# Another order of five engines' work in a kernel of gated linear attention and a feed-forward layer

## The chip, the cores and the metric

The kernel runs on one core of one Trainium2 chip. A core has five engines, each with its own instruction queue that runs in order: TensorE (PE, matmuls into PSUM), VectorE (DVE), ScalarE (ACT, activations by table), GpSimd (POOL) and SyncE (SP, which here only issues transfers). ACT can issue transfers too. The engines wait for one another through semaphores. The metric is the device time of one execution in microseconds.

## The reference

A linear attention with a complex decay, over 4 batches, 8 heads, 768 steps and heads of 48, and then a feed-forward layer over 3072 tokens of 384 with a hidden width of 2048:

```python
scale = np.minimum(mag, 0.999) / (mag + 1e-06)       # mag = |a|
for t in range(S):
    S_re, S_im = ar*S_re - ai*S_im + k[t] v[t]^T, ar*S_im + ai*S_re
    y[:, :, t] = np.einsum('bhd,bhde->bhe', q[:, :, t], S_re)
h = x @ w_in                                          # x: y with the heads side by side
g = h * np.tanh(softplus(h))
return g @ w_out
```

## The kernel before

The work is cut into 12 units of 256 tokens (three to a batch), each unit into two chunks "a" and "b" of 128. A unit goes through three stages.

*Elementwise* (`elementwise`, from line 330 on): loads R and I (the parts of a), Q, K and V. It takes size, logarithm and angle of a, sums them along time (by matmuls with a triangular matrix in units 0 and 1, "mag sum" and "phase sum", lines 404 to 414; by scans on DVE in later units), and forms exp, sine and cosine. "size" (L465) adds two squares, "slope" is L466, "turns" rounds the phase. "grow" multiplies q and k by the magnitudes, "turn sin" and "turn cos" (L545) by sine and cosine. Then twelve relays (L552, six a chunk: sin0 to sin2 and cos0 to cos2) move X and QK through DMAs into T, where heads lie as the matmuls want them.

*Attention* (`attention`): per chunk "kn" (transposes, L608) with "kn out" (L613), "am" (q times k, L620) with "am out" (the mask, L627, DVE only), "y" (L638) with "y out" (L643), "hold" (L668) and "pd" (L651) with "S add" for the state. Then "x move" (L701) brings y by DMA to x, and from unit 1 on "xH" (L712) and "xL" (L717) split it into two parts.

*Feed-forward* (`moe`): eight pairs of 256 hidden columns a unit. For a pair, "mm1" (L746) makes ph, then exp, cap (L815), square, ln, inv on ACT and DVE, "gate" (L759), "gh" (L765) and "gl" (L771) on ACT and DVE, and "mm2" (L783) adds to po. "o" (L794 on ACT, L796 on DVE) scales the result, and "store" writes it. Unit 0 has plain float32 products in four groups of two pairs, q0 to q3, for each chunk; later units use three products of split operands. PSUM banks are few: three for ph, two for pa (am, kn, pd and the sums share them), two for po.

*Weights*: w0 to w15 come in packed words of 768 KB each (w_in even, w_out odd), three buffers at a time, so the load of w3 waits until w0 is unpacked, and so on. "low", "shift" (L283), "join" (L287) and "carry" (L291) unpack one on ACT and DVE; "high" (L309) and "rest" (L314) split it for unit 1 on.

*Fillers*: 40 operations "spin" (numbers 72 to 111) of two matmuls each (L844) that work on the mask alone and whose result nobody reads.

All of this is first listed as 2434 numbered operations, each with the engines that may run it (`op("AV", name, f)`: the first letter is the default). Then `issue` runs through the list `ORDER`, which gives the sequence of all operations; a letter behind a number (V, A, G, T, S for DVE, ACT, POOL, PE, SP) chooses another engine than the default. Each engine gets its operations in this sequence, and the semaphores follow from the data. So `ORDER` alone sets what stands behind what in every queue: also behind which wait a DMA issue stands on SP. The core of it:

```python
for i, other in order:
    engines, name, f = self.ops[i]
    e = other or engines[0]
    assert e in engines
```

Numbers that come up below: 7, 10, 11 and 12 are unit 0a's two squares, size and slope, 24 to 29 those of 0b; 49 and 53 "u0a turn sin" and "turn cos", 50 to 52 and 54 to 56 its relays; 65 to 67 and 69 to 71 those of 0b; 116 and 118 "u0a am0" and "am1"; 154 and 156 "u0b am out0" and "am out1"; 157 and 158 "u0b y0" and "y1"; 192 + 5i is the load of w of index i, and the next four are its low, shift, join and carry, so that 217 to 221 are those of w5; 566 is the load of V2, 597 to 609 are unit 2's relays.

Of the kernel before, what the change touches and what calls it, by code (L numbers as in the profile page):

```python
# [59 lines left out]
361A 152V 175 160 156 157 176 219 150 569 158 214 356 573 163 161 220 164 172 162 272 213V 360A 357 215 159 358 190  # L60
273 221V 189 216V 191 177 274 165 188 359 575 227 178 275 576 363 276 224 223 366 578 283 277 367 180 362 225 369A 370
282 278 364 226V 232 292 284 365 181 279 179 368 228 572 293 237 375A 182 285 303 371 229 183 230 286 280 376A 372 374
574 234 281 373 231V 287 235 386 242 388 131 302 233V 387 236V 288 389 390 289 446 247 378 392 444 239 290 294 381 391
304 379 295 380A 393 312 238 240 296 291 244 297 305 241V 298 394 430 382 395 442 377 245 385 243 397 383 249 400 248
401 384 299 577 398 246V 252 744 448 300 402 399 306 250 307 313 579 438 251V 308 322 396 580 262 452 565 403 405 314
257 323 404 254 564 253 583 255 406 407 582 315 256 309 409 581 408 436 301 410 594A 316 584 411 317 264 318 412 585
265 263 414 413 586 417 324 418 319 434 415 325 587A 266V 310 420 432 259 423 588 593A 326 333 422 751 431 267 258 421
332 260 743 590 566 424V 342 433 428 327 429 334 592 343 328 589 320 335 425 329 426 311 435 591 427 336 321 596 337
462 269 597 603 463 338 602 344 600 748 330 339 607 268 345 604 331 261V 346 599 749 419 606 270 474 347 605 416 440
340 271V 598 464 601 752 348 475 456 437 458 341 465 349 466 439 756 610 612 350 613 441 476 352 443 486 611 353 467  # L70
609 754 351 750 445 468 753G 757 614 354V 469 454 355 616 932 615 470A 933 498 477 758 608 447 478 487 471 479 595 449
499 480 488 617 621 450 481 619 746 937 759 622 745 618 489 760 490 623 491 761 626 620 500 472 492 482 762 501 511
459 755 483 473 624 493 510 763 451 484 494 453 522 502 764 940 628 625 512 460V 503 523 765 627 504 513 630 629 514
505 515 631 495 524 766 485 632 455 636 767A 496 747 516 525 635 768 526 535 936 527 517 633 497 771 773 634 774A 775A
528 534 506 518A 547 507 536 529 770 546 530 641V 519 508 639V 637 537 772 777 509 538 520 539 531 779 521 640 778 638
642 780 938 532 784 548 643 540 549 785 541 533 550 781 542 551 461 783 644 552 787 457 939 655 786 645 769 543 788
656 942 790 789 553 544 944 1123 776 554 657 953 545 646 555 941 791 793 647 556 943 648 557 792V 794 945 658 954 795
558 649 560V 559 797 946 955 1124 796 782 650 668 659 935 947 948 667 956 561 660 934 949 957A 680 661 651 798 679 669
1128V 1131 802 662 1129 652 804 681 670 799 803 671 805 800 682 806 950 683 808 807 692 684 672 809V 653 958 673 952
810 674 951 1132 812 965A 811 1130 654 961V 685 959 1134 691 801 813 703 693 686 663A 675 815 960 964 1133 814 664 963  # L80
817 962 819 1135 694 716 818 816 967 695 825 704 696 824 715 676 969 974 970 665 697 1136 666 820 975 705 698 687A 822
677 706 717 966 1144 688 823 707 678 1145 977 830 708 976 728 699A 968 709 727 979 1137 710 972 718 689 978 821 719
700 1138 971 690 828V 973 711 729 1139 826 981 1305 831 720 983 980 827 701 829 721 1304 730 1140 731 702 1146 722 832
712 723A 1125 1141 833 1126 844 724 1143 1147 713 834 732 1148 714 984 982V 733 1149 725 1142 835 734 985 1155 1151V
735A 987 986 1152 736 857 1153 845 1150 726 988 836 1312 1309V 737 1154A 846 1157 738 992 739 741V 837 994 740 993
1160 847 838 856 995 1158 848 1156 996 1310 839 1494 997 990 998V 858 840A 859 989 1164 849 999 860 1001 1311 1168 850
868 1314G 861 1169 851 869 1159 1000V 841 1165 881 870 1167 1002 991 742 880 1316 1163 1161 1003 1170 1008 862 1166
1004 1005 1493 1009 871 1313 1006 872 863 1010 873 852 1317 1315 892 874 1011 1171 882 1012G 875 1173 1318 893 1007V
1320 1014 904 883 894 1162 853 1319 905 1013 884 1321 1016 885 842 1306 895 864A 1322 1015 843 1498 1307 886 854 1127
1325 876A 1021 855 865 1499 887 1017 866 1019 888 896 877 906 867 1022 897 1018 1326 1020 917 907 1327 908 878 909  # L90
1172 916 898 1328A 899 879 1174 889 1323 1175 910 1177 918 1176 1501 919 1023 1178 900A 1502G 920 1024 1500 921 1179
1503 1506 1180 1504 1324 1182 1329 1507 1184 911 1332 890 901 922 912 1025 1334 891 1335A 1333 902 1185 1330 1026 903
923 1336A 1331 913 1035 924A 1685 1183 1338 1027 1048 1505 914 925 1514 1345 1036 915 1037 1509 1684 1508 1038 1339
926 1186 1039 1515 1350 1028 927 1340 1510 1029 1351 1047 928 1348 930 1030 1040 1187 1516 929 1517 1049 931 1189 1342
1041 1031 1518A 1347 1032 1059 1181V 1349 1519 1343 1060 1341 1188 1033 1344 1050 1042 1051 1346 1034 1511 1061 1043A
1072 1062 1512 1071 1190 1052 1689V 1191 1044 1063 1053 1192 1064 1054 1352 1520 1055 1193 1692V 1354 1690 1045 1196
1197 1065 1693 1083 1513 1195 1066 1194 1073 1084 1074 1067 1075 1046 1085 1086 1096 1056 1087 1202V 1076 1095 1200V
1198V 1337 1068 1077 1495 1057 1088 1201 1496 1203 1526A 1089 1078 1308 1058 1525A 1199 1097 1353V 1107 1098 1090 1099
1069 1695 1355 1100 1079 1697 1108 1080 1101 1356 1109 1698 1358 1357 1691 1522V 1204 1110 1091A 1524 1523 1205 1070
1359 1694 1111 1081 1521 1102 1361 1699 1360 1363 1365 1364 1206 1082 1112 1366 1092 1103A 1207 1216 1113 1528 1208  # L100
1367 1696 1369 1093 1114 1529 1527 1535 1217 1115A 1362 1094 1368 1104 1537 1209 1229 1370V 1865 1534 1105 1540 1218
1539 1106 1219 1116 1220 1705 1210 1228 1117 1118 1371 1119 1121V 1211 1120 1373 1122 1372 1230 1538 1241 1231 1866
# [968 lines left out]
```

## Time and profile before

| | us |
|---|---|
| median of 3 timed runs (592.98 to 595.51) | 594.56 |
| the profiled execution | 597.63 |
| its span, first to last instruction | 595.9 |
| busy in it: PE | 582.5 |
| ACT | 476.2 |
| DVE | 464.2 |
| POOL | 20.9 |
| share of the 16 DMA engines, main queue | 36.8% |

The span is that of one execution under the profiler. "Busy" is the union of an engine's instructions. An instruction's time is from its start to its end, and neighbours overlap: nine matmuls of mm1 listed at some 281 ns each go by in 1.06 us. "Idle before, releaser" tells how long the engine had stood still ahead of an instruction, and whose semaphore ended that. "Granted clock" is the share of its full clock that PE was given in a stretch. The transfers of one queue are issued in order, about 0.6 us apart on SP, and run side by side once issued.

### The profile page before, as it was taken

To read this page: it belongs to the slowest core of one execution; us is meant where nothing else is said; L and a number is where in the kernel's file an instruction comes from. 1 tells how busy PE (TensorE), PEld (TensorE's weight loads), DVE (VectorE), ACT (ScalarE), POOL (GpSimd) and SP (SyncE) were. 2 spreads that over 40 slices of the span, in tenths; PEclk is the share of its full clock that TensorE was granted. 3 is DMA by queue.
4 is the path that set the end of the run, shared out by engine and by line. 5 is a ranking of instruction groups with operands and counts; after the bars stand their busy time and mean duration, and the time that the engine had idled before them with its cause. 6 is when DMAs were issued, how large, how long until landed. Compare 5 with 4: busy or idle time off the path is not lost.

```text
span 595.9 us, 11915 instructions
## 1 busy us (share of the span) xinstructions
PE 582.5 (98%) x4654; PEld 551.1 (92%) x4654; DVE 464.2 (78%) x823; ACT 476.2 (80%) x766; POOL 20.9 (4%) x37
## 2 busy tenths in 40 slices
PE   8979999999999999999999999999999999999995
PEld 4669788799999999999999999999999999999995
DVE  5888999999999977998578889966887646356351
ACT  8877999999998998978868768968977666565572
POOL 4010010100000010000000000001000000000000
PEclk9999999999999999999999999999999999999998
DMA  8595875414606353153270072072053160001000
GB/s 298 185 286 156 252 258 168 152 55 122 181 25 180 94 144 110 49 156 91 72 221 2 15 204 76 14 202 80 28 170 99 36 190 16 28 2 28 28 0 33
DMA packets 57248, 67.07 MB, mean 113 GB/s; under 512 B 4832, under 2 KB 50272, under 8 KB 57184
## 3 DMA queue, kind: packets, MB, share of 16 engines
q1 hardware_dynamic: 55664, 65.01, 36.8%
q10 hardware_dynamic: 1520, 1.22, 0.8%
q8 instruction: 39, 0.64, 0.4%
q14 instruction: 25, 0.20, 0.1%
HBM read 37.75 MB, written 4.72 MB: 71 GB/s over the span
## 4 chain that ended last, share of the span: by engine, by line
PE 58%; DVE 16%; ACT 12%; DMA 6%; issue 4%; SPq 3%; POOL 0%; DVEq 0%; ACTq 0%; POOLq 0%
PE po L783 22%; PE ph L746 21%; ACT e L172 5%; PE ypsum L638 4%; PE pa L620 4%; PE pd L651 3%; ACT X L172 3%; DMA words<-w_out 3%; DVE g L759 2%; SPq L552 2%; DMA T<-X 2%; PE pkn L608 1%; DVE QK L545 1%; DVE X L545 1%; PE junk L844 1%
## 5 line engine op out<-in xcount | busy, mean ns | idle before, releaser
L172 ACT ACTIVATE e<-e 128x512 f32<-128x512 f32 x192 | 118.2, 627 | 26.4 <-DVE e L815 24.6
L746 PE MATMUL ph<-xH,wh 128*128 128x256 f32 x462 | 132.6, 287 | 0.0
L746 PE MATMUL ph<-xL,wh 128*128 128x256 f32 x462 | 129.7, 281 | 0.0
L746 PE MATMUL ph<-xH,wl 128*128 128x256 f32 x462 | 129.7, 281 | 0.0
L783 PE MATMUL po<-wh,gh 128*128 128x384 f32 x308 | 106.4, 345 | 0.0
L783 PE MATMUL po<-wh,gl 128*128 128x384 f32 x308 | 104.4, 339 | 0.0
L783 PE MATMUL po<-wl,gh 128*128 128x384 f32 x308 | 104.1, 338 | 0.0
L759 DVE SCALAR_TENSOR_TENSOR g<-e,ph 128x512 f32<-128x512 f32 x96 | 65.2, 681 | 40.5 <-ACT e L172 40.0
L746 PEld LDWEIGHTS ph<-xH,wh 128*128 128x128 f32 x462 | 87.1, 189 | 0.6
L746 PEld LDWEIGHTS ph<-xL,wh 128*128 128x128 f32 x462 | 87.0, 188 | 0.5
L746 PEld LDWEIGHTS ph<-xH,wl 128*128 128x128 f32 x462 | 87.0, 188 | 0.0
L172 ACT ACTIVATE e<-ph 128x512 f32<-128x512 f32 x96 | 56.4, 590 | 35.9 <-PE ph L746 29.7
L771 DVE TENSOR_TENSOR gl<-g,gh 128x512 fp32r<-128x512 f32 x88 | 60.2, 686 | 14.4 <-PE po L783 9.5
L172 ACT ACTIVATE e<-e,fifth 128x512 f32<-128x512 f32 x96 | 68.9, 720 | 1.2
L815 DVE TENSOR_SCALAR e<-e 128x512 f32<-128x512 f32 x96 | 40.0, 419 | 25.6 <-ACT e L172 25.4
L783 PEld LDWEIGHTS po<-wh,gh 128*128 128x128 f32 x308 | 57.9, 188 | 0.4 <-issue 0.4
L783 PEld LDWEIGHTS po<-wh,gl 128*128 128x128 f32 x308 | 57.9, 188 | 0.3 <-DVE gl L771 0.2
L783 PEld LDWEIGHTS po<-wl,gh 128*128 128x128 f32 x308 | 57.9, 188 | 0.0
L170 ACT ACT_TABLE_LOAD x42 | 53.9, 1283 | 0.7
L620 PE MATMUL pa<-T 96*128 96x128 f32 x384 | 48.7, 276 | 0.4 <-DMA T<-X 0.4
L620 PEld LDWEIGHTS pa<-T 96*128 96x128 f32 x384 | 46.2, 191 | 1.3 <-issue 0.8
L627 DVE TENSOR_TENSOR am<-pa,cmask 128x512 f32<-128x512 f32 x48 | 32.7, 685 | 10.3 <-PE pa L620 10.1
(138 smaller groups left out, 1053.1 us busy)
## 6 DMA issues: line engine op xcount, KB each, us to landing
T<-X SPq DMA_DIRECT2D x68, 129.0 KB, 2.7
T<-QK SPq DMA_DIRECT2D x68, 129.0 KB, 2.5
words<-w_in SPq DMA_DIRECT2D x8, 768.0 KB, 6.5
words<-w_out SPq DMA_DIRECT2D x8, 768.0 KB, 7.1
QK<-k SPq DMA_DIRECT2D x12, 384.0 KB, 5.2
QK<-q SPq DMA_DIRECT2D x12, 384.0 KB, 4.4
V<-v SPq DMA_DIRECT2D x12, 384.0 KB, 4.8
R<-a_re SPq DMA_DIRECT2D x12, 384.0 KB, 3.9
```

The lines of the kernel that those rows point to most:

```text
L170: self.nc.scalar.preload_act_table_set(need)
L172: return self.nc.scalar.activation(out, in_, func, **kw)
L545: e.tensor_tensor(both(st[dst], g)[..., :C], both(st["QK"], g)[..., :C], t.unsqueeze(2).broadcast_to([P, t.shape[1], 2, C]), ALU.mult)
L620: e.matmul(d["pa", g][:, i, :], T()[:, 4 * g + i, 1, :C], T()[:, 4 * g + i, 0, :C], start=True, stop=True)
L627: e.tensor_tensor(d["am", g], d["pa", g], cmask.unsqueeze(1).broadcast_to([P, 4, C]), ALU.mult)
L638: e.matmul(ypsum[64 * par:64 * par + D, i, :], lhs, rhs, start=m == 0, stop=first or m == 1)
L651: e.matmul(d["pd", g][:, i, :], d["kn"][:, h, :], st["V"][:, c, h * D:(h + 1) * D], start=not held, stop=not held or i == 3)
L746: e.matmul(ph[k][:, slot(k, j, a), :], win(x, j, kt, a), st[y][:, kt, cols(k)], start=n == 0, stop=n + 1 == len(todo))
L759: e.scalar_tensor_tensor(g_[k], e_[k], 2.5, ph[k], ALU.subtract, ALU.mult)
L771: e.tensor_tensor(gs[k][1], g_[k], gs[k][0].bitcast(F32), ALU.subtract)
L783: e.matmul(po[t], x[:, slot(k, j, a), 0 if halved else t * P:C if halved else (t + 1) * P], wout(y, j, a), start=j == 0 and a == 0 and n == 0,
L815: op("V", f"{n} cap", lambda e, k=k: e.tensor_scalar_min(e_[k], e_[k], math.exp(20.0)))
```

## The change

The list `ORDER` is another permutation of the same 2434 operations. Nothing else differs. The new list comes from a search that took the service time of every transfer as 1.3 times what a trace had shown. 170 of the operations are given to another engine than before (75 from ACT to DVE, 63 from DVE to ACT, 14 from POOL to DVE, 7 from DVE to POOL, 5 from ACT to POOL, and three DMA issues each way between SP and ACT). The diff replaces the whole list; its beginning, which holds the start of unit 0, and its end:

```diff
 ORDER = [(int(x.rstrip("VAGTS")), x.lstrip("0123456789")) for x in """
-72 0 1 73 2 127 74 3 75 128 7V 5 8 76 4 9 10 77 192 12 11G 197 78 24V 202 13 79 80 132V 25 81 166V 82 27V 19 14 28G 83
-22 15 84 167 85 133 86 169V 16 17 87 170G 135V 26 18 31 32 29G 134 23 88 21 89 20 90 46A 91 33 136 92 42 137 93 94 34
-45 35 30 43V 193 194 95 47A 195 44 96 37 97 49 98 99 196V 50 100 168 36 51 53 139 38 199 55A 56 101 62 60 102 140 54
-103 61A 52 39 104 40 105 6 48 204 57 106 207 41 107 200 138 562 108 58 64 116 59 141 203V 112 114 205 118 117 67A 109
-63 68 110 66A 120 65A 119 69 71A 113V 121 563 206V 115 123 70A 198V 125 217 122 209 111 142 124 210 185A 143 208 126
-201V 187A 144 171 184A 212 567V 129 146 149 211V 145 186 147A 153 570V 130 568 148 151 222 218V 173 155 571G 154 174
...
-2404 2416 2405A 2422 2394 2384 2423 2424 2395 2406 2425 2426 2396 2417A 2427 2407 2418 2428 2408 2429A 2419 2430 2336
-2420 2431 2432 2433A
+72 0 1 73 127 4 74 128 75 2 7 3 76 8 10V 5 11 77 192 14 197 78 9 202 15 12 79 16 132V 80 17 133 81 13 82 83 18 24V
+166V 25 135V 84 19 20 85 22 134 86 27V 21 28 87 88 46 23 31 89 136 32 90 45 167 91 26 92 33 93 29 42 137 34 47A 30 43V
+49 44 36 139 194 53 94 35 39 56 48 140 40 168 54 169V 193V 95 38 51 96 199 142 97 50 41 200 37 98 57 52 99 62 195 100
+55 101 6 60 102 203 562 103 171 104 58 196V 105 61A 138 106 172 64 207 116 59 204 67A 112 68 114 66A 118 117 70A 69
+107 205 71A 563 120 113 119 65A 123 206V 198 108 115V 217 141 170 125 567V 121 124 201V 109 173 143 122 126 212 209
+185A 208V 144 186A 210 146 211V 145 149 184A 153 147 570 148 110 150V 174 155 63 154 187A 129 360G 219 151 176 130 157
+361 156 568 220 158 152 569 571 160 159 111 218V 575 163 190 573 164 222 175 161 213V 188 576 214 273 189 356 165 215
...
+2421 2415 2405A 2384 2423 2424 2395 2406 2425 2416 2396 2417A 2426 2407 2418 2427 2408 2428 2429 2419 2430 2336 2420
+2431 2432 2433A
 """.split()]
```

Per engine, read off the two lists: on PE 148 of the 615 places hold the same operation, and no operation of unit 0 or 1 stands more than nine places from where it was among PE's first 120. SP's queue around unit 2's relays was 597, 602, 600, 607, 604, 599, 606, 605, 598, 601 and is 598, 597, 605, 606, 599, 604, 608, 609, 932, 566, 600, 602, 607, 353, 601.

More of the change, by code (lines that the diff above doesn't have):

```diff
@@ L63 @@
[L63 to L102, printed above, removed]
@@ new lines @@
+891 1178 901 1500 1035 1026 1334 1182 1027 1179 1503G 1336A 1183 1332 1180 920 1335A 1028 1184 1338 921 1187 922 1036
+1181 912 1029 1330 1337 913 902 1333 923 1504 903 914 924A 1505 925 915 1037 1345 926 1185 1684 927 1038 1186G 1189
+928 1506 929 1047 1339 930 1030 1344 1039 1048 1514 1515 1507 931 1351 1060 1188 1049 1347 1031 1508 1050 1308 1059
+1032 1051 1348 1190 1052 1191 1346 1509 1040 1192 1041 1033 1042 1043 1061 1193V 1053 1071 1510 1195 1034 1196 1062
+1044 1063 1194 1072 1516 1054 1064 1349 1517 1342 1045 1073 1340 1065 1074 1083 1341 1055A 1066 1075 1197 1518 1084
@@ new lines @@
+1220 1535 1533 1696 1117 1209 1118 1374 1540 1701 1532 1229 1221 1536 1210 1375 1222 1119 1121V 1376 1211 1120 1539
+1378 1702 1230 1530 1377 1380 1241 1231 1386 1212 1232 1531 1223 1240 1233 1122 1213 1537 1224A 1381 1253 1242 1865
+1225 1234 1384 1243 1252 1704 1705 1534 1706 1244 1214 1385 1391V 1235 1538 1215 1236A 1497 1245 1541 1226 1237 1254
+1383 1246 1255 1264 1870V 1256 1707 1247 1257 1227 1379 1703 1686 1392 1265 1258 1866 1715G 1716G 1687 1871 1259 1276
+1248A 1260 1708 1389 1277 1266 1709 1289 1387V 1278 1390 1710 1238 1267 1279 1268 1288 1249 1280 1388 1281 1382 1239
@@ new lines @@
+1609 1474 2068 1737 1608 1588 1598 1589 1464 1475 1486 1599 1476 1898 1899 1600 2069 1487 1573 1488 1906 1902 1869
+1738 1489 1901 1601 1743 1490 1739 1590 1900 1740 2064 1909 1491V 1741 2066 1591 1745 1744 1602 1748 1746 1747 1750
+2070 1910 1610 2075 2071 1592A 1621 1907 1908 1603 1620 1611 1905 1604A 1749 1742 1904 1632 1751 1612 1912 1593 1622
+1633 1492 1613 2072 2245 1911 1614 1594 1623 1753 2076 1624 1625 1752 2077 1615 1605 1634 1913 1754 2078 1915 1645
+2073 1757 1635 1626 1903 1644 1616A 1627 2246 1636 1756 1595 2074 1758 1637 1606 1755 2087G 1628 1638 2056 1657 1646
@@ new lines @@
+2057 1647 1656 1617 1639 1607 2079 1658 1761V 1648 1763V 1618 1629 1649 1659 1668 1650 1759 1651 1660 1619 2086 2253
+2250V 1760 1661 1630 1762 2080 1662 1631 2251 1764 1663 1669 2252 1640 1916V 1914 1641 1765 2083 2254 1670 1917 1652A
+1664 1671 1919 1672 1918 2258 2081 2255 1642 1673 1920 1766 1643 1767 1768 1921 1769 1922 1674 1924 2082 1926 1925
+1653 1778 1927 1665 1928 2085 1930 1929 1654 1931 2257 1932 2089 1934 1655 1675 2092 1933 1676A 2091 1666 2084 1677
+2090 2266 1777 2267 2256 1667 1779 1770 1780 1678 2268 1781 2269 1923 1679 1935 1771 2096 1790 1680 1782 1681 1789
@@ new lines @@
+1970 1962 1980 2132 1971 1981 1991 2138 1963 1972 2285 1982 1990 1973 2282 1983 2136 1964 1992 2137 1984 1965 2332
+2330 1985 2281 1974 2003 1993 2292 2143V 1994 1975 2249 2002 1995 2135 2284 2014 2004 2287 1996 2005 1976 2290 2141V
+2006 1997 2289 1986A 2015 2007 2288 2008 2291 2026 2016 2009 1998A 2027 2142 2144 2139V 2131 1977 1987 2028 2029 2038
+2017 2030 2140 2018 1999 1988 2010A 2019 1989 2020 2021 2000 2022 2133 2001 2011 2134 2293 2329 2295 2294 2145 2031
+2032 2146 2033 2039 2296V 2034A 2012 2040 2041 2297 2023 2042 2043 2299 2147 2013 2044 2045 2157 2035 2333 2158 2046
@@ new lines @@
+2024 2159 2160 2170 2298 2025 2036 2047 2300 2037 2048 2049 2304 2050V 2302 2305 2148 2149 2301 2052 2150 2306 2053
+2051 2151 2309 2307 2152 2311 2310 2153A 2161 2169 2154 2303 2308 2181 2312 2171 2162 2172 2155 2163 2173 2164 2182
+2174 2193 2175 2183 2314 2165A 2184 2176 2185 2313 2186 2156 2187 2188 2194 2315V 2316 2206 2195 2317 2196 2319 2205
+2166 2318 2334 2177 2218 2207 2178 2197 2320V 2167 2189A 2198 2168 2199 2200 2217 2190 2179 2321 2219 2322 2220 2180
+2323 2201 2208 2230 2209 2202 2210 2229 2211 2221 2191 2212 2324V 2213A 2325 2192 2231 2222 2232 2338 2233 2223 2337
```

104 lines of the change are left out of this document (55 added, 49 removed), and 3 rows, old and new, of the table ORDER.

## The prediction

> **What bounds the kernel now.** I read the page first, then the busy time by stretches, the waits of TensorE (PE), and the chain of waits in order of time.
>
> ```profile
> span 595.9 us, 11915 instructions
> PE 582.5 (98%) x4654; PEld 551.1 (92%) x4654; DVE 464.2 (78%) x823; ACT 476.2 (80%) x766; POOL 20.9 (4%) x37
> ```
>
> PE is the engine that is full. The table by stretches (columns: stretch, its length, then busy us and count for PE, weight loads, DVE, ACT, POOL, then the granted clock and the DMA share) shows where it is not:
>
> ```profile
> 0.00:30.00 30.00, 27.91 (x152) 16.15 (x152) 22.28 (x45) 24.85 (x41) 7.08 (x25) 1.00 0.73 242
> 30.00:60.00 30.00, 26.59 (x241) 24.83 (x240) 26.00 (x48) 21.95 (x38) 1.55 (x1) 0.94 0.74 221
> 60.00:120.00 60.00, 59.12 (x450) 49.01 (x450) 58.82 (x92) 59.25 (x96) 3.73 (x2) 1.00 0.65 204
> 120.00:580.00 460.00, 459.37 (x3769) 451.92 (x3764) 353.99 (x636) 365.55 (x586) 8.55 (x9) 1.00 0.31 88
> 580.00:596.00 16.00, 9.50 (x54) 9.18 (x53) 3.07 (x6) 4.60 (x8) 0.00 (x0) 0.86 0.09 31
> ```
>
> PE is idle for 2.1 us before 30 us, 3.4 us from 30 to 60, 0.9 us from 60 to 120, 0.6 us in the next 460 us, and 6.5 us at the end, after its last matmul. That is 13.5 us in all, and 582.5 + 13.5 is the span within rounding. So three quarters of the kernel have almost nothing to give, and the 6.5 us at the end hold no PE work. What an order can win lies in the first 120 us. What holds PE there:
>
> ```profile
> PE pd L668 <- DVE am L627: 2.3, 1, 2.3
> PE junk L844 <- POOL cmask L226: 1.7, 1, 1.7
> PE psum L404 <- ACT X L172: 1.0, 1, 1.0
> PE ph L746 <- DVE g L759: 0.6, 2, 0.3
> PE pkn L608 <- DMA T<-X: 0.5, 1, 0.5
> PE pa L620 <- DMA T<-X: 0.4, 1, 0.4
> PE pkn L608 <- DMA T<-QK: 0.4, 1, 0.4
> ```
>
> Busy time is not all useful time, though. The page's group of the filler matmuls, and pieces of the chain of waits with equal work at two times:
>
> ```profile
> L844 PE MATMUL junk<-cmask 128*128 128x512 bf16 x80 | 21.4, 424 | 1.7 <-POOL cmask L226 1.7
> ```
>
> ```profile
> 42.46 3.28 PE ypsum L638 x32
> ...
> 167.59 1.79 PE pa L620 x16
> ...
> 172.55 1.90 PE ypsum L638 x32
> ...
> 308.85 1.05 PE po L783 x6
> 309.91 1.06 PE ph L746 x9
> ```
>
> The filler takes 21.4 us, all of it before 33 us. The 32 passes of y take 3.28 us at 42 us, and 1.90 us later on: 1.4 us lost inside "busy". The reason stands in the stretches just there:
>
> ```profile
> 39.00:42.00 3.00, 0.69 (x6) 0.41 (x4) 1.54 (x4) 2.98 (x7) 0.61 (x1) 0.98 1.06 357
> 42.00:44.00 2.00, 2.00 (x18) 1.59 (x18) 2.00 (x5) 1.99 (x5) 0.00 (x0) 0.50 1.16 350
> ```
>
> PE was idle for 2.3 us and came back at a granted clock of 0.50.
>
> **The change, part by part.** No operation is added or removed. All 40 fillers remain, and so do 42 table loads on ACT (counted along the new order). So PE's work is the same, and I price only gaps and clock.
>
> *The end: nothing.* The last nine operations of PE are the same in the same order, and gate, gh and gl of the last pair stay ahead of them. The 6.5 us remain.
>
> *The wait of 2.3 us at 41.67.* DVE stood idle before one weight operation, with the masking of unit 0's second chunk queued behind it:
>
> ```profile
> 40.46 0.56 DVE L279 TENSOR_SCALAR words<-words 128x768 int32<-128x768 uint32 x1 [2.31 <-DMA words<-w_out]
> 40.93 0.68 DVE L627 TENSOR_TENSOR am<-pa,cmask 128x512 f32<-128x512 f32 x1
> ```
>
> The landing of w5 released it. In the new order "u0b am out0" (154) stands ahead of every operation on w5, so y0 can run. But "w5 shift" (219) stands between it and "am out1" (156): the wait for w5 moves to y1 rather than vanishing. PE has y0 in between (16 passes, at 59 ns by the 1.90 us for 32: 0.95 us). Gain: at most 2.3 + 1.4 us of clock, at least nothing. I take 2.0.
>
> *The start of unit 0.* The relays of its first chunk (T<-X, T<-QK) are issued by SP, and PE waits for their last one:
>
> ```profile
> 19.91 1.30 SPq L552 DMA_DIRECT2D T<-X  x2
> 21.65 1.19 SPq L552 DMA_DIRECT2D T<-QK  x2
> 22.88 0.61 SPq L552 DMA_DIRECT2D T<-X  x1
> ```
>
> ```profile
> 21.88 3.61 PE L844 MATMUL junk<-cmask 128*128 128x512 bf16 x16
> 25.88 1.13 PE L620 MATMUL pa<-T 96*128 96x128 f32 x8 [0.38 <-DMA T<-X]
> 26.84 0.82 PE L608 MATMUL pkn<-identity,T 96*128 96x96 f32 x8
> 27.50 1.08 PE L620 MATMUL pa<-T 96*128 96x128 f32 x8
> 28.43 1.03 PE L844 MATMUL junk<-cmask 128*128 128x512 bf16 x4
> ```
>
> Before, two sine relays go while "turn cos" is still computed, ACT issues one cosine relay, and SP has three left (1.8 us). In the new order two cosine relays head SP's queue and the sixth is SP's too: six issues of 0.6 us, 3.7 us, all behind "turn cos". That is 1.9 us later for an equal "turn cos". Against it, DVE has w0's join and carry (0.95 us each, as the row of L287 at 951 ns below) moved behind "turn cos", and three half sums of squares and a slope leave POOL for DVE:
>
> ```profile
> L465 POOL TENSOR_TENSOR X<-X 128x384 f32<-128x384 f32 x3 | 3.0, 988 | 5.8 <-ACT X L172 4.7 <-DVE X L458 1.1
> L466 DVE TENSOR_TENSOR I<-I,X 128x384 f32<-128x384 f32 x3 | 1.7, 551 | 1.7 <-ACT X L172 1.7
> L287 DVE SCALAR_TENSOR_TENSOR w<-words,w 128x768 uint32<-128x768 uint32 x16 | 15.2, 951 | 0.0
> ```
>
> That is 0.4 us less for each sum. The loads of the second chunk (R0, I0 "12") fall behind R1 and Q0, so ACT meets its logarithm later, ahead of the sine and cosine. I take am0 1 us later, between 1 earlier and 3 later. Two fillers that stood ahead of am0 now come behind it (0.45 us each: eight in 3.61 us), so PE has up to 2 us idle ahead of am0 where it had 0.38. By the 0.50 above, such a gap can halve the clock for the 16 passes of am (1.79 us at full) and more: 0 to 2 us. I take 0.5, as the clock fell in one gap of this size and the fillers end close before.
>
> [...]
>
> *What DVE takes over.* 170 operations change engine; DVE goes from 785 to 804 of them, ACT from 729 to 712, POOL from 16 to 14. With
>
> ```profile
> L465 DVE TENSOR_TENSOR X<-X 128x768 f32<-128x768 f32 x7 | 6.7, 953 | 0.1
> L796 DVE TENSOR_SCALAR o<-po 128x384 f32<-128x384 f32 x6 | 3.3, 548 | 2.8 <-PE po L783 2.8
> L712 DVE CAST xH<-x 128x256 fp32r<-128x256 f32 x15 | 4.0, 285 | 0.1
> ```
>
> net five sums (three halves at 551 ns, two whole at 953) make 3.6 us, four o's 2.2, six xH 1.7, and turns, slopes and squares about 3, less some 3 for three kn outs, two gh and one y out at similar lengths: about 8 us more on DVE and less on ACT. After 120 us DVE has 106 us free, and it costs nothing. From 60 to 120 us DVE is idle for 1.2 us only, so there more work means later results: the gates of units 0 to 2 have some 3 to 5 us more DVE work ahead of them than before. The cover is DVE's idle time before 60 us, 7.7 + 4.0 us. Cost between 0 and 3.8; I take 0.7, as most of the extra work stands before 30 us, where the idle time is.
>
> *Unit 2's relays.* Before, SP mixes twelve relays of both chunks:
>
> ```profile
> 99.57 2.69 SPq L552 DMA_DIRECT2D T<-X  x3
> 102.36 1.34 SPq L552 DMA_DIRECT2D T<-QK  x2
> ...
> 105.69 1.25 SPq L552 DMA_DIRECT2D T<-X  x2
> ```
>
> "sin1" of the first chunk is issued at 105.69, and PE waits 0.5 us for it. The new queue has the six of the first chunk ahead of the others; V2 falls nine places behind, and the first pd of unit 2 needs it. Gain 0 to 0.9 (the three DMA rows of PE's waits are 1.3 together, one of them unit 0's): I take 0.5.
>
> *After 120 us.* I counted, for all 96 pairs, the matmul time listed between the last mm1 and the first mm2 (1.06 us a piece): median 17.5 before and 18.2 after; the smallest is the last pair's 7.4 in both, and the next go from 10.3 to 8.5 (unit 11's pairs 2 and 1). The last pair runs through 7.4 with no wait of PE, so 8.5 will do. Other distances, from relay to kn, from S add to the next kn, change both ways. Old loss 0.6 us; new between 0 and 5; I take 1.2, thus 0.6 more, because so many waits were just met before and have been dealt anew.
>
> *Sum:* −2.0 + 1.0 + 0.5 + 0.7 − 0.5 + 0.6 = +0.3 us, nothing. The profiled execution took 597.63 us, with a span of 595.9; the median of the three timed runs is 594.56, 3.1 below it. I put the sum on the median and, as each of the two largest gains has its upper end above what I took, round to **594.3 us**.
>
> **Rivals.**
>
> *Faster: the gaps of the first 120 us close* (waits of 2.3 + 1.0 + 1.3 us and 1.4 us of clock: 6 us at most). For it: each of them is a wait for a transfer or for something queued behind one, and the new order puts weight work later and compute that feeds PE earlier. Against: w5 still stands ahead of y1, and the relays are issued later. With 3.5 to 6 of it: 588.5 to 591, say 590.
>
> *Slower: DVE is the bound from 60 to 180 us.* Its place is the gates of units 0 to 2; its price is the 3.8 us of work put ahead of them; it decides if the new order doesn't start DVE's dense stretch at least that much earlier. For it: 58.82 of 60 us busy. Against: 11.7 us idle before. With the am0 delay: 594.6 + 3.8 + 1 = 599.4.
>
> *The late part loses.* Small waits of 0.3 us, as on "ph <- DVE g", at twenty places: +6 us, 600. Against: 0.6 us in 460 us before.
>
> *The change doesn't do what it says.* It gives transfers more time, but after 120 us no transfer holds PE (DMA share 0.31), so the time given has no use: 594.6, the forecast again.
>
> **How the numbers follow.** Forecast (with the last rival): 0.48. Faster rival: 0.30. DVE rival: 0.14; late losses 0.08. Half a per cent is 3.0 us, about what a measurement of this kernel can tell from none. So faster 0.30, same 0.48, slower 0.22. The range goes from 588.5, the faster rival with nearly all gaps closed, to 599.5; the forecast's own is 591.6 to 597.5.
>
> **What would show it.** PE's idle time by stretches: before 120 us between 4 and 8 us where it was 6.4; the wait of "pd L668" on "am" gone, and one of "ypsum" on "am" in its place. A first am0 after 26 us, with a clock below 1.00 in that stretch if the gap halves it. DVE busy near 472 us, ACT near 470. 120 to 580 us: PE idle below 2 us; above 4 the late part was wrong. The tail after the last matmul at 6.4 us; anything else there would make the forecast wrong by as much.

## The result, and the profile after

The new order is slower: 600.48 us at the median of four runs (599.84 to 602.16) against 594.01 for four of before (592.98 to 595.51), a ratio of 1.0105 with an interval of 1.0076 to 1.0134. Run again with more rounds, it gave 598.68 against 594.24, 1.0070 (1.0044 to 1.0096). So it costs between 4 and 6.5 us, where the prediction said nothing. The profiled execution took 602.16 us.

The head of its page: the span, then busy us and instructions of each engine.

```profile
span 600.4 us, 11890 instructions
PE 582.4 (97%) x4654; PEld 550.8 (92%) x4654; DVE 470.7 (78%) x842; ACT 471.3 (78%) x749; POOL 15.3 (3%) x35
```

PE's busy time is what it was (582.5). What grew is its idle time, 18.0 us for 13.5, and that is the whole difference of the two spans, 4.5 us. The table by stretches (stretch, length, busy us and count of PE, weight loads, DVE, ACT, POOL, then granted clock and DMA share) tells where:

```profile
0.00:30.00 30.00, 25.50 (x132) 15.66 (x133) 21.06 (x44) 23.95 (x41) 2.90 (x21) 0.94 0.59 198
30.00:60.00 30.00, 26.16 (x243) 23.06 (x243) 26.52 (x48) 21.44 (x33) 0.19 (x1) 1.00 0.81 244
60.00:120.00 60.00, 58.38 (x438) 48.55 (x438) 58.17 (x94) 57.10 (x92) 2.93 (x2) 1.00 0.68 214
120.00:580.00 460.00, 458.47 (x3767) 450.32 (x3764) 359.15 (x649) 360.56 (x572) 9.23 (x12) 1.00 0.31 88
580.00:600.40 20.40, 13.84 (x85) 13.24 (x83) 5.81 (x11) 8.25 (x15) 0.00 (x0) 0.89 0.08 24
```

PE is idle for 4.5 us before 30 us (2.1 in before), 3.8 from 30 to 60 (3.4), 1.6 to 120 (0.9), 1.5 to 580 (0.6) and 6.6 at the end (6.5). More than half of the 4.5 us is lost in the first 30 us, where the clock is at 0.94 as well. Single executions differ: each order was profiled once more (before_again and after_again), and there PE is idle for 3.0 and 4.5 us before 30 us, 2.7 and 2.0 to 60, 2.2 and 0.1 to 120, 1.2 and 2.2 to 580. Only the first 30 us and the stretch behind 120 us lose in both pairs.

PE's waits in the whole span (engine, line, releaser: total us, times, longest) have new names:

```profile
PE psum L409 <- ACT I L172: 2.8, 1, 2.8
PE pkn L608 <- DMA T<-QK: 2.2, 2, 1.1
PE junk L844 <- POOL cmask L226: 1.7, 1, 1.7
PE pkn L608 <- ACT e L172: 1.6, 1, 1.6
PE pa L620 <- DVE R L429: 1.4, 1, 1.4
PE psum L404 <- DVE S L660: 0.8, 1, 0.8
```

The wait of "pd L668" on "am" is gone, as forecast. (The row of 1.6 us names ACT, but it stands at 66.67 us ahead of unit 1's first kn, and what that waits for are two relays, which landed at 66.36 and 66.54.) The largest is now one of 2.8 us, and PE's timeline shows it together with what stands behind it (start, us, engine, line, operation; in brackets the idle time before it and its releaser):

```profile
11.15 4.05 PE L844 MATMUL junk<-cmask 128*128 128x512 bf16 x18
17.98 0.49 PE L409 MATMUL psum<-turn,I 128*128 128x128 f32 x2 [2.79 <-ACT I L172]
...
20.61 0.63 PE L404 MATMUL psum<-turn,X 128*128 128x128 f32 x2
...
22.84 5.34 PE L844 MATMUL junk<-cmask 128*128 128x512 bf16 x24
28.02 1.06 PE L620 MATMUL pa<-T 96*128 96x128 f32 x8
```

L409 is "u0b phase sum" (operation 36), L404 "u0b mag sum" (35). The new list puts the phase sum eight places earlier on PE, in front of the magnitude sum and seven fillers. It has to wait for u0b's arctan on ACT, which ends at 17.9 us. That is only 0.3 us later than in before (17.6); there the phase sum came at 20.54 and found its input ready. Everything behind it moves: the magnitude sum ends at 23.0 us (18.1 before). Before, 28 filler matmuls stood on both sides of the phase sum, between 17.95 and 25.5 us; now 24 of them run in one row behind it, from 22.84 to 28.18. Only then can "u0a am0" start. It starts at 28.02 us with no idle time before it: the relays that it needs had landed (the last at 26.15).

Three stretches of 3 us around the gap (same columns as above) show what else it costs:

```profile
15.00:18.00 3.00, 0.21 (x2) 0.02 (x1) 1.94 (x6) 2.97 (x7) 0.00 (x0) 1.00 0.11 47
18.00:21.00 3.00, 3.00 (x16) 2.57 (x17) 3.00 (x7) 2.94 (x5) 0.00 (x0) 0.68 0.03 5
21.00:24.00 3.00, 3.00 (x18) 2.39 (x17) 2.54 (x6) 1.31 (x4) 0.00 (x0) 0.75 0.59 153
```

After 2.8 us without a matmul PE comes back at a clock of 0.68 and 0.75, so the work of these 6 us takes 1.7 us longer than at a clock of 1.00. In before the clock is 1.00 in all of these stretches.

The second loss is on SP. Its queue in the new kernel, then one row of its waits:

```profile
23.65 0.60 SPq L552 DMA_DIRECT2D T<-QK  x1
24.29 0.59 SPq L382 DMA_DIRECT2D V<-v  x1
30.98 0.33 SPq L370 DMA_DIRECT2D R<-a_re  x1
31.42 0.54 SPq L273 DMA_DIRECT2D words<-w_out  x1
32.06 0.60 SPq L552 DMA_DIRECT2D T<-QK  x1
32.71 0.64 SPq L370 DMA_DIRECT2D I<-a_im  x1
33.44 0.50 SPq L273 DMA_DIRECT2D words<-w_out  x1
```

```profile
SPq L370 <- DMA T<-X: 6.1, 1, 6.1
```

The load of R for unit 2 ("R2 load 2", 562) stands still until a relay of unit 0b (T<-X, "u0b relay sin2", issued on ACT's queue at 28.59) has landed, at 30.96. Nothing in R2 needs that relay. The instruction waits on one semaphore only, 107, and it is the one that this relay had used just before. In the traces of before and after, the 302 transfers carry eight DMA semaphores among them (101 to 108, 37 or 38 transfers each), and none of the 294 that follow another on the same semaphore went out before that one had landed; the closest went out 0.02 us behind the landing. In before R2's load carries 107 as well, but the transfer ahead of it there was a relay of u0a that had landed at 24.11, and it went out at 24.67. SP stood for as long in before, and for a relay as well (sin2 of u0b, landed at 31.44):

```profile
SPq L552 <- DMA T<-X: 6.3, 1, 6.3
```

What stood there was u0b's relay cos0; the loads of w3 and R2 had gone out ahead of it. So it is not the stand that is new, but which transfers are caught behind it. Behind R2 on SP stand w3's load (31.42 for 24.23) and u0b's relay cos0 (32.06 for 31.50). (w3's load also waits for w0's carry, which ends at 27.7 us in the new order and at 20.7 in before, so only the time behind that is the stand's.) All of them now run side by side; that relay takes 8.2 us to land where it took 2.5, and PE waits 1.1 us for it. On DVE two operations wait for these loads, and unit 0's "S add" and a phase stand behind them:

```profile
34.92 0.96 DVE L452 SCALAR_TENSOR_TENSOR X<-R 128x768 f32<-128x768 f32 x1 [1.17 <-DMA R<-a_re]
...
39.53 0.56 DVE L283 TENSOR_SCALAR w<-words 128x768 uint32<-128x768 uint32 x1 [2.24 <-DMA words<-w_out]
```

The second is on w3, which landed at 39.51. Those are the 0.8 us ("psum" on "S") and the 1.4 us ("pa" on R) of PE's waits above.

### The profile page after: what moved, and what is told of

It is laid out like the page before. It is cut to its first block, busy times and chain, and to the rows that moved or that the text cites. A ratio compares the mean times of both kernels' runs of the same rounds, so it can differ in the third digit from the quotient of the medians.

```text
span 600.4 us, 11890 instructions
## 1 busy us (share of the span) xinstructions
PE 582.4 (97%) x4654; PEld 550.8 (92%) x4654; DVE 470.7 (78%) x842; ACT 471.3 (78%) x749; POOL 15.3 (3%) x35
## 4 chain that ended last, share of the span: by engine, by line
PE 74%; ACT 12%; DVE 6%; DMA 3%; issue 2%; SPq 2%; POOL 0%; ACTq 0%; DVEq 0%; POOLq 0%
PE po L783 28%; PE ph L746 26%; PE ypsum L638 6%; PE pa L620 6%; ACT e L172 4%; PE pd L651 4%; PE pkn L608 2%; ACT X L172 2%; ACT L170 2%; PE junk L844 1%; DMA words<-w_out 1%; DMA T<-QK 1%; ACT wh L309 1%; ACT R L172 1%; SPq L701 1%
## 5 line engine op out<-in xcount | busy, mean ns | idle before, releaser
L765 ACT CAST gh<-g 128x512 fp32r<-128x512 f32 x46 | 28.1, 613 | 10.4 <-DVE g L759 10.3
```

Source lines behind the costliest of these rows:

```text
L765: (e.copy if e is nc.scalar else e.tensor_copy)(gs[k][0], g_[k])
```

## The experiments

Each kernel ran beside before on the same chip. Two readings are given besides the ratio. For every execution the span and the mean granted clock are known; I call span x (1 - clock) **what the clock took** and span x clock **the rest**, and give the medians. The clock has three digits, so either is good to about 0.3 us for one execution. Before has 1.8 to 2.4 and 590.7 to 591.1 in all five sessions. The two readings need care. In the traces of before and after the clock is at 1.00 or 0.50, and ahead of the last matmul each has one fall of 3.4 us, which is 1.7 us lost. In the tables by stretches of the other 18 profiles the losses from 15 to 50 us add up to nothing, 1.7, 3.4 or 5.1 us (in f_half_late to 3.9, with 0.50 still standing from 45 to 50). One more fall begins 1.9 us behind the last matmul in before and 2.0 in after, where it delays nothing; it makes up 2.2 and 2.3 us of what the clock took. In the other profiles span x (1 - clock) less the losses up to 50 us leaves 0.6 to 2.5 us. So a shift of about 1 us from one reading to the other may come from the end alone.

| kernel | median, us | before beside it | ratio (95%) | clock took | rest |
|---|---|---|---|---|---|
| after | 600.48 | 594.01 | 1.0105 (1.0076 to 1.0134) | 3.6 | 595.5 |
| after_again | 598.68 | 594.24 | 1.0070 (1.0044 to 1.0096) | 2.7 | 594.9 |
| h_after_then_before | 599.86 | 595.26 | 1.0082 (1.0056 to 1.0108) | 3.6 | 594.6 |
| h_before_then_after | 597.44 | 595.26 | 1.0052 (1.0025 to 1.0079) | 1.5 | 594.2 |
| f_half_late | 597.09 | 594.56 | 1.0048 (1.0025 to 1.0070) | 2.4 | 593.6 |
| e_phase | 598.96 | 595.26 | 1.0055 (1.0029 to 1.0081) | 1.8 | 595.6 |
| e_late | 598.17 | 594.54 | 1.0059 (1.0037 to 1.0081) | 2.1 | 594.2 |
| e_start | 600.44 | 594.54 | 1.0101 (1.0080 to 1.0123) | 4.2 | 594.5 |
| e_both | 599.03 | 594.54 | 1.0080 (1.0052 to 1.0108) | 5.1 | 592.0 |
| f_relay | 599.74 | 594.56 | 1.0075 (1.0049 to 1.0101) | 3.3 | 594.7 |
| f_all | 599.23 | 594.56 | 1.0074 (1.0048 to 1.0101) | 4.8 | 592.9 |
| g_r2 | 596.35 | 594.08 | 1.0030 (1.0009 to 1.0052) | 1.2 | 593.2 |
| g_all | 597.12 | 594.08 | 1.0039 (1.0020 to 1.0059) | 1.5 | 593.7 |
| a_nofill | 598.29 | 594.24 | 1.0063 (1.0042 to 1.0085) | 6.3 | 590.9 |
| b_nofill | 595.59 | 594.24 | 1.0017 (0.9998 to 1.0037) | 4.2 | 589.7 |
| b_phase | 597.13 | 594.56 | 1.0038 (1.0012 to 1.0065) | 3.0 | 592.2 |
| b_w5 | 594.27 | 595.26 | 0.9982 (0.9957 to 1.0008) | 1.5 | 591.2 |
| b_relays | 593.77 | 594.24 | 0.9982 (0.9966 to 0.9998) | 1.8 | 590.1 |

Before itself was profiled once more (596.02 us, span 594.2), which comes last. Where a loss or gain against before is given in us below, it is the ratio's, on 594.5 us.

### Which part of the list: two halves

The list was cut at unit 0's first mm1 (about 47 us).

```diff
 h_before_then_after: before's ORDER up to the first of operations 272, 273; what is left in after's order
 h_after_then_before: after's ORDER up to there; what is left in before's order
```

> The order of before up to the first mm1 of unit 0 (47 us), the changed order from there on. Theory (the loss arises at the start, and the rest only carries it): 594 to 595. Rival (2 us arise at the start, the rest later, as the starts of equal places of PE in the two traces say: 2.0 us at the first mm1, 3.4 at the first transposes of unit 1, 4.3 at the end): 598 to 598.5.

> The changed order up to the first mm1 of unit 0, the order of before from there on. Theory (loss at the start): 599.5 to 600.5. Rival (only 2 us at the start): 596.

The first 47 us in the new order cost 4.9 us with before's order behind them, most of the whole loss. In the trace the first mm1 stands at 49.8 us; after has 49.4 and after_again 49.1, before 47.4 in one profile and 44.9 in the other. The other half costs 3.1 us by the timed runs, with no more taken by the clock. Its trace shows less: the first mm1 is at 44.8 and the end at 595.0, 0.8 us behind that of before profiled again. The halves add up to 8 us by their ratios, more than the whole; a list joined from two has a seam, and what it costs is not known.

### The phase sum

```diff
 after, with operation 36 (u0b phase sum) behind 35 (u0b mag sum)
-43V 49 44 36 139 194 53 94 35 39 56
+43V 49 44 139 194 53 94 35 36 39 56
```

> The changed order with one operation moved: u0b phase sum stands behind u0b mag sum in PE's queue instead of nine places ahead of it. Theory (the fillers are on the path: the phase sum waits 2.95 us with 14 fillers queued behind it, so they end 1.9 us after the last relay of u0a has landed): first am0 at 26.2 instead of 28.0 us, and the total 1.5 to 2 us less, 598.5 to 599. Rival (the next wait, of kn0 of u0b for a relay that SP issues behind the load of w3, takes its place): am0 earlier, first mm1 where it was, total 600.0 to 600.5.

PE's timeline of this kernel has the sums at 16.45 to 19.4, and am0 is on time again:

```profile
16.45 0.49 PE L404 MATMUL psum<-turn,X 128*128 128x128 f32 x2 [1.19 <-DVE X L478]
...
19.26 5.34 PE L844 MATMUL junk<-cmask 128*128 128x512 bf16 x24
25.85 1.13 PE L620 MATMUL pa<-T 96*128 96x128 f32 x8 [1.24 <-DMA T<-X]
```

The wait and the late am0 are gone, and with them the fall of the clock at 19 us, which all five profiles with the gap of 2.8 us show and none of the others. In this trace the first mm1 stands at 47.3 us, 2.1 earlier than in after. Over all executions the gain is smaller or lies elsewhere: the clock took 1.8 us as in before, but the rest is at 595.6, as in after. By the ratios it is 0.9 us against after_again and 2.9 against the first comparison. So the phase sum explains 1 to 3 us. What is left in this trace is R2's load, which still stood until 29.75, and another fall of the clock at 35 us (0.66 from 35 to 40).

Its place by itself, in the old list:

```diff
 before, with 36 behind 30 (u0b arctan), then filler 94, then 35
-94 34 45 35 30 43V ... 100 168 36 51
+34 45 30 36 94 35 43V ... 100 168 51
```

> before, with u0b's phase sum at the place that the new list gives it on PE: ahead of one filler, the magnitude sum and the eight fillers behind it. Its arctan ends at 17.6 here (17.9 in after), so PE would wait 1.4 us, not 3. If the fillers behind the wait are what makes unit 0's first am0 late: am0 0.9 to 1.4 us later (near 27), magnitude sum 19.2 or later, and 0 to 1 us on the total, as w5's wait of 1.7 to 2.3 us stands behind it. If a wait of PE there is worth what after lost by it: 2 us or more.

The gap was 1.5 us and am0 came at 26.8 us, 0.9 later than in before, as worked out. Yet the cost is 2.3 us (0.7 to 3.9), of which the clock took 0.6. In the trace the price shows later, at u1a's sum on PE and, ahead of it, on ACT (one row of each timeline):

```profile
36.44 2.49 PE L404 MATMUL psum<-less,X 128*128 128x128 f32 x12 [3.14 <-ACT X L172]
```

```profile
35.29 0.59 ACT L643 COPY y<-ypsum 112x512 f32<-112x512 f32 x1 [4.10 <-DMA T<-X]
```

ACT stood 4.1 us ahead of a relay that it issues itself ("u0b relay cos1"), until another, sin1, whose semaphore it shares, had landed at 34.65; in before profiled again the same thing held ACT until 31.98 and PE for 1.2 us. So the old order pays for shared semaphores as well. Here sin1 ran beside the loads of w3 and R2, which went out half a microsecond later than in before profiled again (24.7 and 25.1 for 24.1 and 24.6) and took 8.3 and 9.0 us where they had taken 5.0 and 6.3. Whether that is the phase sum's doing, one profile can't say; the 2.3 us are from twelve executions.

### The relay that I thought was late

Two edits were tried first for the second loss: u0b's relay cos0 ahead of the loads of R2 and w3, without and with three fillers moved in front of am0.

```diff
 e_start: e_phase, and 69 right behind 68, then 562 and 207 behind it; fillers 107, 108, 109 ahead of 116
 f_relay: the same without the fillers
```

> The changed order with u0b phase sum behind u0b mag sum, three fillers (107 to 109) ahead of am0 again, and u0b relay cos0 ahead of the loads of R2 and w3 on SP. Theory (the start is lost to the order of PE and SP, not to the work that DVE took over): first mm1 at 45 to 46 us, total 1 to 2.5 us above before. Rival (DVE's 4 us of added work before the gates of units 0 to 2 is the bound once the start is mended): first mm1 as said, but the first transposes of units 1 and 2 no earlier than 64.2 and 109.3 us, the total 3.3 above before as with the phase sum alone.

> After, with u0b's phase sum behind its magnitude sum (as in e_phase), and SP's second relay of u0b (cos0) moved ahead of the loads of R2 and w3, which wait for w0's carry; the fillers stay where they are. For each execution I split the span into what the clock took, span x (1 - granted clock), and the rest, span x clock: medians before 1.8 to 2.4 and 590.7, after 3.6 and 595.5, e_phase 1.8 and 595.6. If the loss before unit 0's first mm1 is the phase sum and the relay behind those loads: mm1 near 45 to 46 us (47.3 in e_phase), rest near 593, total 1 to 2 us above before. If the loss lies in DVE's work (am1 and u1a's sums wait for DVE there) or in the clock: mm1 stays at 47 or more, total at e_phase's +3.3.

Both missed. In f_relay PE no longer waited for that relay, but the relay, now the next transfer in order, stood in R2's place for the same semaphore of sin2 until 30.77. R2's load went out behind it, at 31.41, and DVE and PE waited longer for it. (SP's relays went out 1.0 us late in this execution, the first at 20.91 for 19.88 in e_phase, so the rows overstate the effect.)

```profile
35.92 0.96 DVE L452 SCALAR_TENSOR_TENSOR X<-R 128x768 f32<-128x768 f32 x1 [2.35 <-DMA R<-a_re]
```

```profile
37.21 2.32 PE L404 MATMUL psum<-less,X 128*128 128x128 f32 x12 [2.00 <-DVE S L660]
```

DVE's 1.17 us of waiting had become 2.35, PE's 0.81 had become 2.00. That pointed to R2's load rather than to the relay. In e_start the clock went down too, once PE had no filler between 30 and 40 us (the table by stretches):

```profile
30.00:35.00 5.00, 3.39 (x24) 2.77 (x24) 2.67 (x6) 4.01 (x6) 0.00 (x0) 0.69 0.93 255
35.00:40.00 5.00, 3.83 (x18) 3.84 (x19) 4.97 (x9) 1.24 (x4) 0.00 (x0) 0.50 1.02 388
```

### R2's load

The next edit takes R2's load out of that stand, by issuing it when SP is idle, ahead of all relays.

```diff
 g_r2: e_phase, with operation 562 (R2 load) ahead of 56 (u0a relay cos2)
-35 36 39 56 48 ... 203 562 103
+35 36 39 562 56 48 ... 203 103
```

> e_phase (after, u0b's phase sum behind its magnitude sum), with R2's load ahead of all relays on SP, where the queue is idle from 7.5 to 20 us. In after R2's load stands at 30.98 us, 0.02 us behind the landing of u0b's relay sin2 on the other queue, whose semaphore (107) it waits for; w3's load and u0b's relay cos0 stand behind it on SP; DVE waits 1.2 us for R2 and PE behind that. If this wait is what the start still loses after the phase sum: no wait of DVE for R, V0's load lands as before, first mm1 1 to 2 us earlier than e_phase's 47.3, and the total from e_phase's +3.3 to +1 to +2. If w3's load (still issued near 31, as its buffer and the sine relays hold it) or the clock is: mm1 47 or later, total at +3 or more.

SP's queue, and the DVE operation that had waited:

```profile
7.67 0.33 SPq L370 DMA_DIRECT2D R<-a_re  x1
19.89 1.31 SPq L552 DMA_DIRECT2D T<-QK  x2
...
23.84 0.59 SPq L382 DMA_DIRECT2D V<-v  x1
29.80 0.33 SPq L273 DMA_DIRECT2D words<-w_out  x1
```

```profile
32.46 0.95 DVE L452 SCALAR_TENSOR_TENSOR X<-R 128x768 f32<-128x768 f32 x1
```

DVE's wait is gone, its work begins 2.5 us earlier than in after, the first mm1 stands at 45.4 us (47.3 in e_phase), and the clock is 1.00 from 15 to 50 us. SP stands as before: w3's load, now the next in order, waits 5.3 us for sin2 and goes out at 29.80 (30.19 in e_phase). The total is 1.8 us above before by the ratio (0.5 to 3.1) for e_phase's 3.3 (1.7 to 4.8), with the rest at 593.2 for 595.6. The edit does two things at once: R2 no longer stands, and its 384 KB no longer run beside w3's load, which took 5.7 us to land for 7.2. No run tells the two apart. By ratios two places, one group of matmuls and one load, carry 2.4 of after_again's 4.2 us, or 4.4 of the first comparison's 6.2.

### The late wait

In the new order PE waits 1.1 us at 455 us for a relay of unit 10. Five kernels were made with and without it:

```diff
 e_late: after, operation 2098 (u10a relay cos1) behind 2101 (u10b relay cos1) on SP
 e_both, f_all, f_half_late, g_all: the same in e_start, f_relay, h_before_then_after, g_r2
```

```profile
455.32 0.85 PE L608 MATMUL pkn<-identity,T 96*128 96x96 f32 x8 [1.10 <-DMA T<-QK]
```

> The changed order with one DMA issue moved: u10a relay cos1 stands behind u10b relay cos1 on SP, 13 issues earlier, ahead of the load of V10 and four relays of the second chunk. Theory (this relay, landing 5.0 us after its issue beside them, holds u10a kn0): PE's wait of 1.3 us at 455 us goes, the total is 1.3 us less, about 5 us above before. Rival (the matmuls it frees wait for the next thing): the wait goes and the end stays, 6.2 above before.

> Both edits together. If they add up: 0 to 1.5 us above before. If the late wait is taken over by another: as with the start alone.

> f_relay, with u10a's last relay (cos1) behind u10b's on SP as in e_late... that is, at the place where PE doesn't wait for it at 455 us. If the three named places (phase sum, relay of u0b, relay of u10a) are the whole loss: within 1 us of before, rest near 591.5. If the list loses in many small places: 2 to 3.5 us above before.

> before's order up to unit 0's first mm1 and after's behind it, with the relay of u10a mended as in e_late. h_before_then_after took 3.1 us more than before with a clock loss no larger (1.5) and a rest of 594.2, though its trace shows mm1 as early as before's (44.8) and only 0.8 us more behind it than before_again's. If the one wait of 1.0 to 1.3 us at 455 us is the late loss: +1.8 to +2.1, rest 593. If nothing changes (+3): the late loss lies elsewhere, and the trace of one execution doesn't show it. If it falls to +1 or less: the wait costs more than it shows in a trace.

> g_r2 and u10a's last relay behind u10b's on SP, as in e_late. If the three named places are the loss: 0 to +1.5 us against before, with the rest (span x clock) near 592. If the list loses in many places none of which is named: +2 to +3.5. Against g_r2 it tells once more what the wait at 455 us is worth (1.0 to 1.3 by the trace).

The row is gone from the edited traces (their unedited partners have 0.2 to 1.1 us there), but the totals hardly tell: by the ratios 0.1 to 1.2 us less in four pairs (e_late against after_again, e_both against e_start, f_all against f_relay, f_half_late against h_before_then_after) and 0.5 more in the fifth (g_all against g_r2), each within its intervals. The rest fell by 0.7, 2.5, 1.8 and 0.6 us and rose by 0.5, in the same sequence: 1.0 less in the mean. That agrees with the row and doesn't prove it. f_half_late at +2.9 and g_all at +2.3 are misses of the theory that three places are all: the order behind the first mm1 costs some 2 us that no row of a trace names.

### The fillers

```diff
 a_nofill: after; fillers 95 to 102 issue nothing
 b_nofill: before; fillers 107 to 111 issue nothing
```

These leave out 16 and 10 matmuls whose result nobody reads.

> The changed kernel, unchanged, on the chip of the next three, for a second profile and a closer ratio. Theory (a gap of 2.95 us at 15 to 18 us, a fall of the clock behind it in each execution, 3.3 us lost by the first mm1 and 1.2 more in the second half): 4.5 to 6 us above before, with PE's clock below 1.00 between 18 and 25 us. Rival (the first profile was an unlucky execution): clock 1.00 there and the first mm1 near 47 us.

> The changed order, with eight of the fillers (95 to 102), which stand between u0b phase sum and u0a am0, issuing nothing: 16 matmuls less, 3.4 us at full clock. Theory (there they are the last thing ahead of am0, which starts 1.9 us after the landing of its last relay): am0 at 26.2 to 26.5 instead of 28.0, the total 1 to 2 us less than the changed kernel. Rival (fewer fillers let the clock fall once more, as in the run with the start mended, 0.50 from 35 to 40 us): the total equal or more.

> The order of before, with the last five fillers (107 to 111: two ahead of am0, two ahead of y0, one ahead of u1a mag sum) issuing nothing. Theory (they keep the clock up between 25 and 45 us, where PE waits in four places): a clock well below 1.00 in 30 to 45 us, 1 to 3 us more than before. Rival (they are neutral, as PE waits there anyway): equal within 0.5 us.

a_nofill on PE's timeline, and one stretch of its table:

```profile
26.18 1.13 PE L620 MATMUL pa<-T 96*128 96x128 f32 x8 [1.28 <-DMA T<-X]
```

```profile
35.00:40.00 5.00, 5.00 (x25) 3.78 (x25) 3.99 (x8) 1.04 (x3) 0.00 (x0) 0.51 1.03 364
```

am0 starts at 26.18 and waits for its relay again, and the rest is 590.9, 4.0 less than after_again's: 16 matmuls at 0.22 us (5.34 for 24) are 3.6 us, so about all of it was on the path. But the clock took 6.3 us in place of 2.7, with 0.51 from 35 to 40 us. Before, robbed of five of its fillers, gained 1.0 in the rest and lost 2.4 to the clock. So in the old order the five fillers may earn a little (1.0 us by the ratio, with an interval that reaches to nothing), and in the new one the eight about pay for themselves (after_again is 0.4 us slower than a_nofill, within the noise). In these runs the fillers held up the clock (it took 2.7 us with them and 6.3 without eight, 1.8 and 4.2 without five), and those behind the wait were part of the path (3.6 us of matmuls, 4.0 in the rest).

### Parts of the change in the old order

```diff
 b_w5:     before, with 218V (w5 low) behind 156 (u0b am out1)
 b_relays: b_w5, with 232 (w8 load) behind 368 (u1a relay cos0) and 602, 600, 607 (u2b) behind 598 (u2a relay sin1)
 before_again: before
```

> The order of before with one operation moved: w5 low stands behind u0b am out1 in DVE's queue instead of ahead of u0b am out0. Theory (PE's wait of 2.3 us at 41.7 and the 1.4 us at a clock of 0.50 behind it are what w5 costs before): 590.5 to 592. Rival (the next wait takes its place, for the mover of x or for w6): 593.5 to 594.5.

> The order of before with w5 low behind u0b am out1 (as in an earlier run, 1.1 us below before), and on SP the load of w8 behind u1a's last relays and unit 2's second-chunk relays behind its first-chunk ones. Theory (PE's waits for relays of 0.8 to 2.1 us at the first transposes of unit 1 and 0.95 at those of unit 2 go): 2 to 3 us below before. Rival (w8, landing later, holds DVE, which is full from 60 us on): 0.5 to 1.5 below before, or none.

> The kernel before, unchanged, for a second profile. If the slow clock behind PE's wait of 2.3 us at 41.7 comes in only some executions, this one shows the first mm1 near 44.8 us (as in the run with the start of before and the rest of the changed order) and not 47.4; if it comes in each, 47.4 again.

These take from the new order what the prediction counted as gains. Both gained less than was expected (some 2.6 to 4 us and 2 to 3). b_w5 gains 1.1 us with an interval that reaches to a loss of 0.5; its PE had no wait on "am" and reached the first mm1 at 43.1 us. b_relays is the one version whose interval stays below 1, by little. Before profiled again shows the wait on "am" with 1.5 us and a clock of 1.00 behind it: the fall to 0.50 after 2.3 us belonged to that one execution.

## Why the prediction was wrong

**The step that failed is the start of unit 0**: "I take am0 1 us later", and 0.5 us for the clock. am0 was 2.1 us later (28.02 for 25.88), which lies within the bounds given, but not for the reason given. The relays were not late; the last one landed 0.4 us later than before. The phase sum was, with fillers behind it. I compared each engine's list by how far operations had moved and stopped at "no operation stands more than nine places from where it was". Eight places were enough: the phase sum changed sides with operations whose inputs were there, its own input came at 17.9 us in the new order and at 17.6 in the old, and everything behind it on PE waited. The late loads of the second half had been noticed ("ACT meets its logarithm later, ahead of the sine and cosine"), but they were worth 0.3 us at the arctan; what counted was the place of the operation that waits for it. The sign given for this step, a first am0 after 26 us with a clock below 1.00, came true and would have misled: the fall was ahead of am0, not in a gap before it.

**The second miss is a wait that I did not look for.** w0's carry behind "turn cos" was priced as DVE time saved, and not as the release of w3's load. What SP's queue holds behind V0, R2's load first, was not followed; and that a load can wait for a transfer it has nothing to do with, through a shared semaphore, as R2's did for 6.1 us, was in none of the terms. g_r2 against e_phase puts its price at 1.5 us by the ratios and 2.4 in the rest, with R2's share of the traffic in it.

In the prediction's own sum the terms up to the first mm1 (w5, am0, the clock) make −0.5 us, where h_after_then_before measured +4.9. The terms behind it make +0.8, where h_before_then_after measured +3.1 (1.5 to 4.6): the late part was too small as well, and no row says by what.

Term by term:

- *The end: nothing.* Right: 6.6 us after the last matmul for 6.5.
- *The wait for w5, -2.0.* The wait of "pd" on "am" is gone, as said, and none of "ypsum" on "am" took its place. The gain didn't come: w3's late load put 2.24 us of waiting on DVE in the same stretch, and PE got 1.1 and 1.4 us of new waits ahead of am1. In the old order the same move was worth 1.1 us by the ratio (between a gain of 2.6 and a loss of 0.5). The 1.4 us of clock in the term came with a single execution; before_again has 1.00 there.
- *The start, +1.0 and +0.5.* Mis-sized, with the wrong cause: h_after_then_before gives 4.9 us for everything up to the first mm1, w5's term included.
- *DVE's extra work, +0.7.* The work was counted rightly: DVE and ACT have 470.7 and 471.3 us where 472 and 470 were worked out. That it costs PE anything is not shown. PE's idle time from 60 to 120 us rose from 0.9 to 1.6 us, which looks like the term, but the wait there is for relays, and the second profiles have 2.2 for before and 0.1 for after; that the sizes met is chance. From unit 1's first "kn" to unit 2's the new order takes no longer (66.7 to 111.8 us, 63.3 to 109.0 in before), so the rival that DVE is the bound falls; its time of 599.4 was near for another reason.
- *Unit 2's relays, -0.5.* Right: PE waits 0.5 us ahead of u2a's first kn in both profiles of before and not at all in both of after.
- *After 120 us, +0.6.* Right by the traces (0.6 to 1.5 us idle in the first pair, 1.2 to 2.2 in the second), of which 1.1 us is a relay's in after. The timed runs of h_before_then_after and f_half_late ask for some 2 us more than that.
- *The signs.* PE's idle time before 120 us was to lie between 4 and 8 us; it is 10.0 in after, and 6.6 in after_again, where two falls of the clock hide more of the loss inside "busy".

**The medians.** The sum was put on a median of three runs, while the trace behind it was an execution 3.1 us above. Some 2.2 of the 3.7 us that I saw to gain at w5's wait (1.4 of clock, 0.8 of the wait) were that execution's own: before_again has a wait of 1.5 us there and a clock of 1.00.

**What stays open.** With both named places mended and the late wait too (g_all), 2.3 us above before remain (1.2 to 3.5). Part lies in the start (mm1 at 46.4 us; before 44.9 and 47.4, b_w5 43.1), part perhaps in the late half. One profile per kernel, with executions 2 us apart either way, can't place it.

## What to carry to other kernels

When an order changes, look on each queue not for how far an operation moved but for pairs that changed sides, and ask of the one now in front when its last input comes; what stands behind it pays, on that engine and on those that wait for it. Ask the same of DMA queues: where does the queue stand, for which transfer on the same semaphore, and what is caught behind it? Where a repair gives nothing, split the span into clock and the rest over all executions before believing or dropping it: a_nofill won 4.0 us of the rest and lost 3.6 to the clock. And profile both kernels twice before believing a stretch: from 60 to 120 us the second pair said the opposite of the first.

## What the runs showed of the hardware

- **The clock fell after gaps under 3 us.** A gap of 2.8 us at 15 us took the clock to 0.67 to 0.72 in the stretch from 20 to 25 us in after_again, a_nofill and h_after_then_before, and to 0.68 in the 3 us behind it in after. One of 2.3 us did it in the first profile of before; gaps of 1.5 us (before again at 40 us, b_phase at 16) did not, while in f_half_late, which waits 1.5 us on "am" as well, the clock was at 0.72 from 40 to 45 us.
- **Scattered gaps did it too.** In e_start PE waited no longer than 0.8 us at a time between 29 and 34 us, 1.6 of the 5 us from 30 to 35 together, and the clock was at 0.69 there and at 0.50 in the next 5.
- **A small transfer took three times as long beside large ones.** u0b's relay cos0 of 129 KB lands 2.5 us after its issue in before and 8.2 us after it in the new order, issued 0.6 us behind a load of 768 KB. A relay of unit 1, issued between two such loads, took 7.5 us (58.89 to 66.36).
- **The clock moved the total in steps.** In before and after it is at 1.00 but for one fall to 0.50 ahead of the last matmul, at 41.9 and at 19.0 us, of 3.4 us each, and one behind it. By the tables by stretches, the clock takes 1.7 us from 15 to 50 us in e_phase, e_late, b_phase, f_relay and g_all, 3.4 in after_again, h_after_then_before, e_both, b_nofill and f_all, 5.1 in a_nofill and e_start (there in one row, from 32 to 42 us), and nothing in g_r2, before_again, b_w5, b_relays and h_before_then_after.
